# Spectral layer with routed experts: row stores of the last batches spaced out, a first table of twenty tiles, one layout of the first matrix

## The chip, the cores and the metric

One core of a Trainium2 chip runs the whole program. The metric is the device time of one execution in microseconds (us). The kernel before takes 1574.06 us, the median of three runs (1569.97 to 1574.5). Engines are named as in the profile: PE does matrix products, ACT and DVE work on whole tiles, POOL sends rows by indirect DMA, SP issues the other DMAs.

## What is computed

Two layers follow each other. The first transforms eight batches of 2496 tokens and 256 columns along the tokens, mixes the columns in the frequency domain, shrinks the result by 0.01 and transforms back. The second picks one of eight experts for each token and applies two matrices of that expert.

```python
X = np.fft.rfft(x, axis=1)
Yr = Xr @ w_r - Xi @ w_i + b_r
Yi = Xr @ w_i + Xi @ w_r + b_i
...
y = np.fft.irfft(Y, n=x.shape[1], axis=1)
...
expert_idx = np.argmax(x @ w_gate, axis=1)
h = np.maximum(xe @ w1[e], 0.0)     # 256 -> 1024
out[mask] = gate_w[mask, None] * (h @ w2[e])
```

## The kernel before

The program has two stages that overlap a little. In the **spectral stage** (`spectral`, 80 iterations, ten for each batch) a batch is transformed, mixed and transformed back. `route` then finds, for half a batch at a time, each token's expert and its place in that expert's list in DRAM (`xs_dram`). It leaves a generator of eleven **row stores** in `self.rows`: each is one indirect DMA of POOL (L646) that writes up to 117 rows of 1056 bytes to their places. `send(1)` lets one of them go, and `pace(after)` ahead of it makes POOL copy one number of the tile `after` (`mark`, L577), so that the store waits until that tile is there.

In the **expert stage** the lists are worked off in tiles of 256 rows. `step(t)` is a tile: it issues the load of tile t + 4 (`load`), then `up` multiplies by the first matrix, in four pieces of two column blocks each, and `down` multiplies by the second matrix, in two halves of 128 rows. Every product is three PE matmuls, since numbers are split in a rounded part and a rest. For each piece of `up`, ACT makes `hh` from the sum in PSUM (L923) and DVE makes the rest `hl` (L924); only then is the PSUM buffer free again. The sums have two buffers (pool `psa`) while the inverse transform still holds its share of PSUM, and four from tile `BUSY` on, when `psb` is opened. `down` ends with ACT's `part` (L958), DVE's `o` (L959) and an indirect DMA of POOL to `out` (L961), for each half.

`finish_last` is the seam. It interleaves the inverse transform of the last batch (`inv_a`, twelve steps), the routing of that batch and the tiles 0 to `BUSY - 1`. `step` is a generator that gives way after each piece of `up` and each half of `down` (in tiles 0 and 1 also in the middle of a half), and each time `breathe` does three steps of routing and sends one row store:

```python
def breathe(self, after):
    self.tick(3)
    self.nudge()
    self.pace(after)
    self.send(1)
```

Which expert and which rows a tile has is not known to the program before it runs. `table(0)` computes it for the first `EARLY` tiles, from lists of the first five batches, in which these tiles are already full. So their loads don't wait for later row stores. `table(1)` has all other tiles, and the load of tile `EARLY` (in `step(EARLY - 4)`) waits until every row store has landed. Column 1 of a table says whether a tile has another expert than the one before; then `split1` and `split2` make both matrices anew from `r1` and `r2` (eight ACT copies, L851 and L857, and eight DVE subtractions, L852 and L858), else a branch jumps over them. The first tile of a table always counts as another expert.

The first four tiles (`PLAIN`) have a **layout** of their own. Their rows are loaded by one DMA each into `xw`, and PE turns them with four transposes into PSUM (`px`, L886). From tile 4 on, four DMAs fetch pieces of 256 bytes into `xq`, a fifth fetches weight and token number into `xr`, and DVE turns 32 x 32 blocks (L890). The rows of the first matrix lie in another order for that, so the table also calls for new matrices at tile 4 (the last column of `tcol`), whatever its expert.

The order on PE, ACT, DVE and SP is the order of the code; POOL runs in program order too.

Of the kernel before, what the change touches and what calls it, by code (L numbers as in the profile page):

```python
# [10 lines left out]
F32 = mybir.dt.float32  # L11
# [17 lines left out]
XW = 264  # L29
# [2 lines left out]
OOB = 1 << 20  # L32
RARE = 3
ROUND = 1.5 * 2.0 ** 23
EARLY = 12
PLAIN = 4
BUSY = 8


def constants(nb):  # L40
    n1 = np.arange(NA)
    n2 = np.arange(NB)
    k2 = np.arange(NB)
    fa = np.zeros((117, 120))
    fe = np.zeros((78, 120))
    ga = np.zeros((120, 117))
    for j in range(3):
        for k1 in range(K1):
            ph = 2 * np.pi * ((n1 * k1) % NA) / NA
            c, r = j * 40 + 2 * k1, slice(j * 39, (j + 1) * 39)  # L50
            for q, v in enumerate((np.cos(ph), -np.sin(ph))):
                fa[j::3, (2 * k1 + q) * 3 + j] = v
                if j < 2:
                    fe[j::2, (2 * k1 + q) * 3 + j] = v
            f = (1 if k1 == 0 else 2) / S
            ga[c, r] = f * np.cos(ph)
            ga[c + 1, r] = -f * np.sin(ph)
    bm = np.zeros((128, K1, 128))
    bi = np.zeros((128, K1, 128))
    for k1 in range(K1):  # L60
        k = k1 + NA * k2
        s = np.where(k > S // 2, -1.0, 1.0)
        th = 2 * np.pi * ((n2[:, None] * k[None, :]) % S) / S
        c, z = np.cos(th), np.sin(th)
        bm[:64, k1, :64] = c
        bm[64:, k1, :64] = z
        bm[:64, k1, 64:] = -z * s
        bm[64:, k1, 64:] = c * s
        live = (((k != 0) & (k != S // 2)) * s)[:, None]
        bi[:64, k1, :64] = c.T  # L70
        bi[64:, k1, :64] = -z.T * live
        bi[:64, k1, 64:] = z.T
        bi[64:, k1, 64:] = c.T * live
    cap = TT + nb * S
    nt = (nb * S + E * (TT - 1)) // TT
    p = np.arange(117)
    g = np.arange(G)
    n2o = p[:, None] // NA + 3 * g[None, :]
    tok = NB * (p[:, None] % NA) + n2o
    ok = n2o < NB  # L80
    ids = np.where(ok[:, None, :], tok[:, None, :] + S * np.arange(nb)[None, :, None], OOB)
    score = np.broadcast_to((8.0 - np.arange(E))[None, None, :], (117, G, E)) * ok[:, :, None]
    base = np.broadcast_to((np.arange(E) * cap + TT)[None, :], (128, E))
    ltri = (p[:, None] < p[None, :]).astype(np.float64)
    tcol = np.stack([np.arange(128.0), np.arange(128.0) - 1, np.where(np.arange(128) == 0, 1.0, 0.0),
                     np.arange(128.0), np.arange(128.0) + 128,
                     np.where(np.arange(128) % PLAIN == 0, 1.0, 0.0) * (np.arange(128) <= PLAIN)], 1)
    return {
        "c_fa": fa.astype(np.float32),
        "c_fe": fe.astype(np.float32),  # L90
        "c_ga": ga.astype(np.float32),
        "c_bm": bm.astype(np.float32),
        "c_bi": bi.astype(np.float32),
        "c_ids": np.ascontiguousarray(ids.astype(np.int32)),
        "c_score": np.ascontiguousarray(score.astype(np.float32)),
        "c_base": np.ascontiguousarray(base.astype(np.float32)),
        "c_ltri": ltri.astype(np.float32),
        "c_tcol": tcol.astype(np.float32),
    }


class Kernel:
# [35 lines left out]
    def open_inverse(self, st, pst):  # L138
        nc, nb = self.nc, self.nb
        cp = self.cp  # L140
# [12 lines left out]
        nc.vector.memset(self.used, 0.0)  # L153
        self.tabs = [cp.tile([1, 4, 128], I32, name=f"tab{i}") for i in range(2)]
        self.drop = cp.tile([128, 128, 2], I32, name="drop")
        self.tcol = cp.tile([128, 6], F32, name="tcol")

        k = self.k = self.pool(st, "k", 1)
        self.wi = self.pool(st, "wi", 3)
# [385 lines left out]
            if next(self.tabling, "wait") == "wait":  # L545
                break

    def breathe(self, after):
        self.tick(3)
        self.nudge()  # L550
        self.pace(after)
        self.send(1)

    def finish_last(self):
        tiles = itertools.chain.from_iterable(self.step(t) for t in range(BUSY))
        fill = itertools.chain(self.first1(), self.first2())
        for i in range(GH + 1):
            self.inv_a(self.nb - 1, i)
            if i:
                self.pace(self.yb[0:1, (2 * i - 1) % GH, 8:9])  # L560
                self.send(1)
            else:
                for _ in self.upright(0):
                    pass
            for _ in range(2 if 0 < i < 3 else 1):
                next(fill, None)
            self.breathe(next(tiles) if i > 2 else self.h1.bitcast(F32)[0:1, 0, 0:1])
        self.jobs.append(self.table(1))
        for after in tiles:
            self.breathe(after)  # L570
        while self.jobs:
            self.tick(1)
        self.send(100)

    def pace(self, after):
        if self.rows:
# [84 lines left out]
    def table(self, last):  # L661
        nc, rt = self.nc, self.rt
# [42 lines left out]
        nc.vector.tensor_scalar_min(fin[:, 0:2], fin[:, 0:2], float(E - 1))  # L705
        nc.vector.tensor_tensor(out=fin[:, 2:3], in0=fin[:, 0:1], in1=fin[:, 1:2], op=ALU.is_gt)
        yield
        nc.vector.tensor_max(fin[:, 1:2], fin[:, 2:3], tcol[:, 2:3] if last else tcol[:, 5:6])
        nc.vector.tensor_scalar(out=te, in0=st0, scalar1=tcol[:, 0:1], scalar2=-1.0, op0=ALU.subtract, op1=ALU.mult)
        yield  # L710
        nc.vector.scalar_tensor_tensor(out=ind, in0=te, scalar=0.0, in1=ge, op0=ALU.is_ge, op1=ALU.subtract)
# [44 lines left out]
    def open_early(self):  # L756
        self.xst.close()
        k2 = self.pool(self.top, "k2", 1)
        self.r1 = [k2.tile([128, F], F32, name=f"r1{q}") for q in range(2)]
        self.r2 = [k2.tile([128, 4, D], F32, name=f"r2{q}") for q in range(2)]  # L760
        self.xws = [k2.tile([128, 2, XW], F32, name=f"xw{t}") for t in range(PLAIN)]
        self.xqs, self.xrs, self.xts, self.hs, self.new = {}, {}, {}, {}, {}
        self.weights(0, 1)
        self.weights(0, 2)
        for t in range(PLAIN):
            self.load(t)

    def open_experts(self, st):
# [13 lines left out]
    def load(self, t):  # L782
        if t >= self.nt:
            return
        nc = self.nc
        row = self.word(2, t, E * self.cap - TT)
        rows = self.xs[bass.ds(row, TT), :]
        tc = self.tc

        def fetch(dst, src):  # L790
            i = nc.sync.dma_start(dst, src)
            if PLAIN <= t < self.early:
                tc.declare_no_dep(i.ins, group="xs", reason="rows of the first batches, behind the first tile's load")
            if t < self.early:
                tc.add_to_no_dep_group("early", i.ins)

        if t < PLAIN:
            fetch(self.xws[t], rows.rearrange("(h p) c -> p h c", h=2))
            self.xrs[t] = self.xws[t]
            return  # L800
        xq = self.w2p.tile([128, 8, 2, 32], F32, tag="xq", name="xq", bufs=5)
        for q in range(4):
            fetch(xq[32 * q:32 * q + 32].rearrange("p t c i -> p t (c i)"),
                  rows[:, 8 + 64 * q:72 + 64 * q].rearrange("(t j) c -> j t c", t=8))
        xr = self.w2p.tile([128, 2, 2], F32, tag="xr", name="xr", bufs=6)
        fetch(xr, rows[:, 0:2].rearrange("(h p) c -> p h c", h=2))
        self.xqs[t], self.xrs[t] = xq, xr

    def weights(self, t, which):
# [3 lines left out]
        e = self.word(0, t, E - 1)  # L813
        ch = self.word(1, t, 1)
        for q in range(2):
            if which == 1 and t < PLAIN:
                parts = [(self.r1[q], self.w1[bass.ds(e, 1), q * 128:(q + 1) * 128, :].rearrange("o p f -> p (o f)"))]
            elif which == 1:
                parts = [(self.r1[q][p * 32:p * 32 + 32],
                          self.w1[bass.ds(e, 1), p * 64 + q * 32:p * 64 + q * 32 + 32, :].rearrange("o i f -> i (o f)"))  # L820
                         for p in range(4)]
# [54 lines left out]
    def upright(self, t):  # L876
        if t >= self.nt:
            return
        nc = self.nc
        if t < PLAIN:  # L880
            xf = self.psb.tile([128, 512], F32, tag="o", name="px") if self.psb else \
                self.psi.tile([128, 512], F32, tag="u", name="px", bufs=4)
            xf = xf.rearrange("p (c h t) -> p c h t", c=2, h=2)
            for c in range(2):
                for h in range(2):
                    nc.tensor.transpose(xf[:, c, h, :], self.xrs[t][:, h, 8 + c * 128:136 + c * 128], self.ident)  # L886
            xf = xf.rearrange("p c h t -> p c (h t)")
        else:
            xf = self.w2p.tile([128, 2, 8, 32], F32, tag="xf", name="xf")
            nc.vector.transpose(xf.rearrange("p c t j -> p t c j"), self.xqs.pop(t))  # L890
            yield
            xf = xf.rearrange("p c t j -> p c (t j)")
        xh = self.w2p.tile([128, 2, TT], F32R, tag="xh2", name="xh2", bufs=2)
        xl = self.w2p.tile([128, 2, TT], F32R, tag="xl2", name="xl2", bufs=2)
        with self.tc.high_priority():
# [6 lines left out]
    def up(self, t, work=()):  # L902
# [8 lines left out]
        for f2 in range(4):  # L911
# [12 lines left out]
                nc.vector.scalar_tensor_tensor(out=hl[:, s, :], in0=p, scalar=0.0, in1=hh[:, s, :],  # L924
                                               op0=ALU.max, op1=ALU.subtract)
            next(work, None)
            yield hh.bitcast(F32)[0:1, f2 * 2, 0:1]
        self.hs[t] = (hh, hl)

    def down(self, t):  # L930
# [12 lines left out]
        for h in range(2):  # L943
# [3 lines left out]
            for f in range(8):  # L947
# [3 lines left out]
                    nc.tensor.matmul(p[:, :D], hl[:, 7, hs], w2[:, 7, 0, :], start=False, stop=False)  # L951
                nc.tensor.matmul(p, hh[:, f, hs], w2[:, f].rearrange("p a d -> p (a d)"), start=f == 0, stop=f == 7)  # L952
                if f == 3 and t < 2:
                    yield hl.bitcast(F32)[0:1, 7, 0:1]
            if not h:
                self.split1(t + 1)
            part = self.w2p.tile([128, D], F32, tag="part", name="part", bufs=2)
# [6 lines left out]
            if t or h:  # L964
                tc.declare_no_dep(i.ins, group="out", reason="every token is in one tile only")
            tc.add_to_no_dep_group("out", i.ins)
            yield part[0:1, 0:1]

    def step(self, t):
        if t + 4 <= self.nt - RARE:  # L970
# [53 lines left out]
```

## Time and profile before

| | before |
|---|---|
| median of three runs | 1574.06 us |
| the profiled execution | 1569.84 us |
| its span, first to last instruction | 1568.1 us |
| PE busy | 1522.0 us (97%) |
| DVE, ACT, POOL busy | 911.2, 781.3, 394.3 us |
| granted clock, mean | 0.992 |

A busy share is a mean over stages. To see what a change in one stage is worth, the stage has to be cut out: here tile by tile, from the first matmul of a tile's `up` to the first of the next tile's. A row of the timeline gives an instruction's start and duration and, in brackets, how long its engine sat idle ahead of it and what ended that.

### The profile page before, as it was taken

The page shows a single profiled execution, that of the slowest core. Times are in us where ns is not written, and L with a number is a line of the kernel's source. Part 1 is how long each engine was busy: PE and PEld are TensorE (multiplying, and loading weights), DVE is VectorE, ACT ScalarE, POOL GpSimd, SP SyncE. Part 2 cuts the span into 40 slices and gives each one's busy share as a digit, 9 for nine tenths or more (in the row PEclk, how much of TensorE's full clock was granted, in tenths as well). Part 3 has the DMA queues.
Part 4 walks back from the last instruction along what each step waited for, and adds up shares of the span by engine and source line. Part 5 has one row for each costly group of instructions (what it writes and reads, how often), then busy time and mean ns, then how long its engine had stood idle before and what let it go on. Part 6 is the DMA issues. An engine that isn't in the chain of part 4 may idle for free. (4 is left out here: it accounts for less than half of the span.)

```text
span 1568.1 us, 35495 instructions
## 1 busy us (share of the span) xinstructions
PE 1522.0 (97%) x10949; PEld 1401.5 (89%) x10950; DVE 911.2 (58%) x2106; ACT 781.3 (50%) x1689; POOL 394.3 (25%) x555
## 2 busy tenths in 40 slices
PE   6999999999999999899999999999999999999997
PEld 3899999999989888789899999999999999999996
DVE  3677787777778776554655445445445445446443
ACT  2667777777777675343443334334334334334332
POOL 1002433416251534631111212111111112111111
PEclk8999999999999999999999999999999999999998
DMA  8864544636453422532433213223123213122110
GB/s 242 227 191 121 167 139 140 182 110 196 118 174 97 132 59 57 157 95 72 124 106 81 67 42 99 49 47 100 46 52 90 56 42 104 44 71 74 46 45 20
DMA packets 188386, 159.96 MB, mean 102 GB/s; under 512 B 122299, under 2 KB 158817, under 8 KB 187918
## 3 DMA queue, kind: packets, MB, share of 16 engines
q1 hardware_dynamic: 168237, 113.46, 28.3%
q0 software_dynamic: 19936, 44.04, 8.4%
q8 instruction: 89, 1.46, 0.4%
q14 instruction: 124, 1.01, 0.2%
HBM read 242.02 MB, written 66.37 MB: 197 GB/s over the span
## 5 line engine op out<-in xcount | busy, mean ns | idle before, releaser
L952 PE MATMUL po<-h,hh 128*128 128x512 f32 x1312 | 462.4, 395 | 0.4 <-ACT hh L923 0.4
L918 PE MATMUL ph<-xh,h 128*128 128x256 f32 x1312 | 372.4, 284 | 8.4 <-DVE hl L924 7.5
L918 PE MATMUL ph<-xl,h 128*128 128x256 f32 x1312 | 371.4, 283 | 0.0
L918 PE MATMUL ph<-xh,l 128*128 128x256 f32 x1312 | 371.0, 283 | 0.0
L949 PE MATMUL po<-h,hl 128*128 128x256 f32 x1148 | 324.1, 282 | 0.9 <-DVE hl L924 0.7
L924 DVE SCALAR_TENSOR_TENSOR hl<-ph,hh 128x512 fp32r<-128x512 f32 x328 | 226.2, 690 | 159.0 <-ACT hh L923 121.2
L961 POOL DMA_INDIRECT out<-o,row x140 | 139.4, 996 | 656.2 <-DVE o L959 539.8
L923 ACT ACTIVATE hh<-ph 128x512 fp32r<-128x512 f32 x328 | 193.9, 598 | 213.0 <-PE ph L918 199.1
L952 PEld LDWEIGHTS po<-h,hh 128*128 128x128 f32 x1312 | 241.4, 188 | 44.3 <-ACT hh L923 0.9
L918 PEld LDWEIGHTS ph<-xh,h 128*128 128x128 f32 x1312 | 251.5, 192 | 9.9 <-DVE hl L924 8.8
L918 PEld LDWEIGHTS ph<-xh,l 128*128 128x128 f32 x1312 | 251.4, 192 | 3.7
L959 DVE SCALAR_TENSOR_TENSOR o<-po,xr,part 128x256 f32<-128x256 f32 x156 | 75.5, 484 | 304.7 <-ACTq L871 155.4
L918 PEld LDWEIGHTS ph<-xl,h 128*128 128x128 f32 x1312 | 251.5, 192 | 0.0
L958 ACT ACTIVATE part<-po,xr 128x256 f32<-128x256 f32 x156 | 73.8, 473 | 335.9 <-PE po L952 324.1
L949 PEld LDWEIGHTS po<-h,hl 128*128 128x128 f32 x1148 | 215.3, 188 | 8.0 <-DVE hl L924 3.7
L646 POOL DMA_INDIRECT xs_dram<-yb,pos x176 | 175.6, 998 | 64.2 <-issue 51.1
L366 DVE SCALAR_TENSOR_TENSOR y<-v,r 64x256 f32<-64x256 f32 x320 | 134.2, 419 | 6.9 <-ACT r L360 0.8
L390 PE MATMUL pz<-iw,z 128*120 128x136 f32 x704 | 97.0, 280 | 1.9 <-DVE zl L396 1.2
L309 PE MATMUL pb<-bm,t 128*128 128x128 f32 x640 | 86.7, 279 | 11.9 <-DMA t<-spec_dram 9.0
L382 ACT COPY z<-pv 128x256 f32<-128x256 f32 x160 | 94.2, 711 | 3.7 <-PE pv L379 1.5
L309 PEld LDWEIGHTS pb<-bm,t 128*128 128x128 f32 x640 | 80.0, 194 | 13.1 <-issue 10.8
L379 PEld LDWEIGHTS pv<-bi,y 128*128 128x128 f32 x640 | 79.8, 192 | 12.2 <-issue 7.7
(188 smaller groups left out, 2550.9 us busy)
## 6 DMA issues: line engine op xcount, KB each, us to landing
r<-moe_w SPq DMA_DIRECT2D x174, 512.0 KB
r<-moe_w SPq DMA_DIRECT2D x640, 128.0 KB
spec_dram<-ae SPq DMA_DIRECT2D x88, 240.0 KB
t<-spec_dram SPq DMA_DIRECT2D x160, 128.0 KB
xq<-xs_dram SPq DMA_DIRECT2D x316, 64.0 KB
x<-x SPq DMA_DIRECT2D x40, 384.0 KB
x<-x SPq DMA_DIRECT2D x40, 84.0 KB
xs_dram<-yb,pos POOLq DMA_INDIRECT x176
```

The lines of the kernel that those rows point to most:

```text
L309: nc.tensor.matmul(p[:, c, :, kp, :], t[:, kp, c * 128:(c + 1) * 128], self.bm[:, 2 * s + kp, :], start=True, stop=True)
L366: nc.vector.scalar_tensor_tensor(out=y[q * 64:q * 64 + 64, kp, :], in0=u[h, q, :], scalar=LAM, in1=r[h, q, :], op0=ALU.add, op1=ALU.min)
L379: nc.tensor.matmul(p[:, c, kp, :, :], y[:, kp, c * 128:(c + 1) * 128], self.bi[:, 2 * s + kp, :], start=True, stop=True)
L382: nc.scalar.copy(self.z[:, c, 0:NB, 4 * s:4 * s + 4].rearrange("p n a -> p a n"), p[:, c].rearrange("p a r n -> p (a r) n"))
L390: nc.tensor.matmul(p[:120, c * 136:(c + 1) * 136], self.z[:, c, 3 * g:3 * g + 3, :].rearrange("p j a -> p (j a)"), self.iw[:, c, :], start ...
L646: i = nc.gpsimd.indirect_dma_start(out=self.xs[:, :], out_offset=bass.IndirectOffsetOnAxis(ap=pos[:n, g:g + 1], axis=0), in_=y[:n, g, 0:XW ...
L918: nc.tensor.matmul(p[:, i, :], a[:, c, f * 128:(f + 1) * 128], v[:, c, :], start=m == 0, stop=m == 5)
L923: nc.scalar.activation(hh[:, s, :], p, AF.Relu)
L924: nc.vector.scalar_tensor_tensor(out=hl[:, s, :], in0=p, scalar=0.0, in1=hh[:, s, :], op0=ALU.max, op1=ALU.subtract)
L949: nc.tensor.matmul(p[:, :D], hl[:, f - 1, hs], w2[:, f - 1, 0, :], start=False, stop=False)
L952: nc.tensor.matmul(p, hh[:, f, hs], w2[:, f].rearrange("p a d -> p (a d)"), start=f == 0, stop=f == 7)
L961: i = nc.gpsimd.indirect_dma_start(out=self.out[:, :], out_offset=bass.IndirectOffsetOnAxis(ap=at[h], axis=0), in_=o[:, h, :], in_offset=N ...
```

## The change

Row stores: `breathe` no longer paces and sends. In `finish_last` one store goes with each step of `inv_a`, as before, and from tile 2 on `up` sends one after its second and one after its fourth piece, in the later part of the program too, until none is left. The `send(100)` at the end of `finish_last` is gone.

First table: `EARLY` is 20 instead of 12, `BUSY` 7 instead of 8.

Layout: tiles 0 to 3 are loaded and turned as all others. `PLAIN`, the four PE transposes of a tile and the call for new matrices at tile 4 are gone; the first load of the first matrix comes in eight DMAs of 128 KB instead of two of 512 KB.

```diff
-EARLY = 12
-PLAIN = 4
-BUSY = 8
+EARLY = 20
+FIRST = 4
+BUSY = 7
...
-    def breathe(self, after):
+    def breathe(self):
         self.tick(3)
         self.nudge()
-        self.pace(after)
-        self.send(1)
...
-            self.breathe(next(tiles) if i > 2 else self.h1.bitcast(F32)[0:1, 0, 0:1])
+            if i > 2:
+                next(tiles)
+            self.breathe()
         self.jobs.append(self.table(1))
-        for after in tiles:
-            self.breathe(after)
+        for _ in tiles:
+            self.breathe()
         while self.jobs:
             self.tick(1)
-        self.send(100)
...
-        nc.vector.tensor_max(fin[:, 1:2], fin[:, 2:3], tcol[:, 2:3] if last else tcol[:, 5:6])
+        nc.vector.tensor_max(fin[:, 1:2], fin[:, 2:3], tcol[:, 2:3])
...
-        if t < PLAIN:
-            fetch(self.xws[t], rows.rearrange("(h p) c -> p h c", h=2))
-            self.xrs[t] = self.xws[t]
-            return
-        xq = self.w2p.tile([128, 8, 2, 32], F32, tag="xq", name="xq", bufs=5)
+        xq = self.xws[t] if t < FIRST else self.w2p.tile([128, 8, 2, 32], F32, tag="xq", name="xq", bufs=5)
...
-        if t < PLAIN:
...
-            for c in range(2):
-                for h in range(2):
-                    nc.tensor.transpose(xf[:, c, h, :], self.xrs[t][:, h, 8 + c * 128:136 + c * 128], self.ident)
-            xf = xf.rearrange("p c h t -> p c (h t)")
-        else:
-            xf = self.w2p.tile([128, 2, 8, 32], F32, tag="xf", name="xf")
-            nc.vector.transpose(xf.rearrange("p c t j -> p t c j"), self.xqs.pop(t))
-            yield
-            xf = xf.rearrange("p c t j -> p c (t j)")
+        xf = self.w2p.tile([128, 2, 8, 32], F32, tag="xf", name="xf")
+        nc.vector.transpose(xf.rearrange("p c t j -> p t c j"), self.xqs.pop(t))
+        yield
+        xf = xf.rearrange("p c t j -> p c (t j)")
...
             next(work, None)
-            yield hh.bitcast(F32)[0:1, f2 * 2, 0:1]
+            if t > 1 and f2 % 2:
+                self.pace(hh.bitcast(F32)[0:1, f2 * 2, 0:1])
+                self.send(1)
+            yield
```

POOL in tile 2, from its second piece of `up` to its second output, before (`mark` is the pacing copy, `xs_dram` a row store, `out` an output; the two branches belong to the skipped matrices):

```order
L577 COPY mark<-hh 1x1
L646 DMA xs_dram<-yb,pos 161792x264
L577 COPY mark<-hh 1x1
L646 DMA xs_dram<-yb,pos 161792x264
L863 UNCONDITIONAL_BRANCH
L577 COPY mark<-part 1x1
L646 DMA xs_dram<-yb,pos 161792x264
L961 DMA out<-o,xw_8082 19968x256
L577 COPY mark<-part 1x1
L646 DMA xs_dram<-yb,pos 161792x264
L961 DMA out<-o,xw_8082 19968x256
```

and with the change, all of tile 2:

```order
L575 COPY mark<-hh 1x1
L644 DMA xs_dram<-yb,pos 161792x264
L575 COPY mark<-hh 1x1
L644 DMA xs_dram<-yb,pos 161792x264
L856 UNCONDITIONAL_BRANCH
L948 DMA out<-o,xi_8086 19968x256 x2
```

A tile has two row stores instead of six; tiles 2 to 13 have them, where before tiles 1 to 4 had.

SP at the end of the spectral stage, the load of tile 0, before:

```order
L780 TENSOR_LOAD tab_76
L780 ISA x2
L791 ISA
L791 DMA xw_8080<-xs_dram 128x2x264
L780 TENSOR_LOAD tab_76
```

and with the change:

```order
L779 TENSOR_LOAD tab_76
L779 ISA x2
L790 ISA
L790 DMA xq_8080<-xs_dram 32x8x64
L790 ISA
L790 DMA xq_8080<-xs_dram 32x8x64
L790 ISA
L790 DMA xq_8080<-xs_dram 32x8x64
L790 ISA
L790 DMA xq_8080<-xs_dram 32x8x64
L790 ISA
L790 DMA xi_8084<-xs_dram 128x2x2
```

One issue became five, for each of four tiles.

DVE in tile 2, after its first piece of `up`, where the rows of tile 3 are turned, with the change (`carry` and `rb` are routing):

```order
L908 SCALAR_TENSOR_TENSOR hl<-ph,hh 128x512
L874 STREAM_TRANSPOSE xf<-xq_8082 128x8x2x32
L626 TENSOR_TENSOR carry<-carry,scan_102 117x8
L628 CAST carry_b<-carry 117x8
L630 SCALAR_TENSOR_TENSOR rb<-pr,base 117x8
L908 SCALAR_TENSOR_TENSOR hl<-ph,hh 128x512
```

The second row is new on DVE; on PE the four transposes of `xw` between two pieces of `up` are gone.

## Rows read from the trace of the kernel before

**Rows 1.** The page: span, and PE's busy time.

```profile
span 1568.1 us, 35495 instructions
PE 1522.0 (97%) x10949; PEld 1401.5 (89%) x10950; DVE 911.2 (58%) x2106; ACT 781.3 (50%) x1689; POOL 394.3 (25%) x555
```

**Rows 2.** Windows: tiles 1 to 5, 7, 11, 12, 16; last, tiles 13 to 80.

```profile
core 0: us, PE busy (x) PEld busy (x) DVE busy (x) ACT busy (x) POOL busy (x), PEclk, DMA share, GB/s
618.14:630.87 12.73, 12.54 (x91) 11.32 (x89) 8.64 (x30) 4.09 (x9) 6.46 (x11) 1.00 0.15 46
630.87:647.38 16.51, 14.04 (x88) 12.75 (x87) 7.65 (x33) 3.71 (x7) 10.78 (x17) 0.90 0.38 106
647.38:663.44 16.06, 13.16 (x91) 11.46 (x90) 9.88 (x30) 5.83 (x11) 9.60 (x14) 1.00 0.75 221
663.44:677.90 14.46, 12.25 (x83) 10.79 (x82) 10.11 (x18) 8.00 (x15) 7.41 (x12) 1.00 0.65 190
677.90:690.92 13.02, 11.61 (x82) 10.69 (x80) 7.25 (x12) 5.82 (x11) 3.17 (x3) 1.00 0.18 42
702.50:714.09 11.59, 11.59 (x81) 10.70 (x80) 4.95 (x8) 3.90 (x7) 2.94 (x3) 1.00 0.20 47
748.14:760.68 12.54, 12.08 (x82) 10.62 (x80) 9.56 (x16) 7.77 (x15) 2.10 (x3) 1.00 0.79 211
760.68:772.20 11.52, 11.52 (x82) 10.67 (x80) 7.22 (x13) 5.60 (x11) 2.89 (x3) 1.00 0.23 57
806.28:817.76 11.48, 11.48 (x81) 10.63 (x80) 7.22 (x13) 5.60 (x11) 2.50 (x3) 1.00 0.20 44
772.20:1545.27 773.07, 773.07 (x5442) 723.67 (x5441) 373.51 (x668) 291.54 (x532) 135.51 (x136) 1.00 0.26 65
```

**Rows 3.** Timeline of PE: instructions that it waited for in tiles 0 to 5.

```profile
598.18 0.38 PE L404 MATMUL py<-zh,gh 120*117 120x272 f32 x1 [1.83 <-ACT yb L405]
...
636.88 0.39 PE L918 MATMUL ph<-xh,h 128*128 128x256 f32 x1 [2.46 <-DVE hl L924]
...
655.00 0.39 PE L918 MATMUL ph<-xh,h 128*128 128x256 f32 x1 [2.02 <-DVE hl L924]
...
668.17 0.38 PE L918 MATMUL ph<-xh,h 128*128 128x256 f32 x1 [1.61 <-DVE hl L924]
...
682.34 0.38 PE L918 MATMUL ph<-xh,h 128*128 128x256 f32 x1 [1.41 <-DVE hl L924]
```

**Rows 4.** Timeline of ACT: `part` in tiles 1 and 6.

```profile
633.71 0.47 ACT L958 ACTIVATE part<-po,xw 128x256 f32<-128x256 f32 x1 [5.00 <-PE px L886]
...
702.76 0.47 ACT L958 ACTIVATE part<-po,xr 128x256 f32<-128x256 f32 x1 [2.33 <-PE po L952]
```

**Rows 5.** Timeline of POOL: row stores at the end of tile 1.

```profile
629.02 0.99 POOL L646 DMA_INDIRECT xs_dram<-yb,pos  x1 [0.17 <-issue]
...
630.38 0.99 POOL L646 DMA_INDIRECT xs_dram<-yb,pos  x1 [0.18 <-issue]
```

**Rows 6.** Timeline of PE: the transposes in tile 0, the table's matmuls in tile 3.

```profile
591.71 0.60 PE L886 MATMUL px<-ident,xw 128*128 128x128 f32 x4
592.15 0.28 PE L390 MATMUL pz<-iw,z 128*120 128x136 f32 x1
...
659.43 1.03 PE L740 MATMUL pq<-ident,fin 128*1 128x128 f32 x8
660.39 0.51 PE L952 MATMUL po<-h,hh 128*128 128x512 f32 x1
```

**Rows 7.** Groups by line: DVE's transposes (busy us, mean ns, idle before).

```profile
L890 DVE STREAM_TRANSPOSE xf<-xq 128x512 f32<-128x512 f32 x79 | 55.4, 702 | 0.0
```

**Rows 8.** Timelines of SP (loads of tiles 0 to 3; a later tile's) and POOL.

```profile
546.81 4.24 SPq L791 DMA_DIRECT2D xw<-xs_dram  x4
...
690.55 1.90 SPq L791 DMA_DIRECT2D xq<-xs_dram  x4
...
565.07 0.34 POOL L577 COPY mark<-k 1x1 f32<-1x1 f32 x1 [18.05 <-ACT k L345]
```

More of the change, by code (lines that the diff above doesn't have):

```diff
@@ L85, in constants @@
     tcol = np.stack([np.arange(128.0), np.arange(128.0) - 1, np.where(np.arange(128) == 0, 1.0, 0.0),
-                     np.arange(128.0), np.arange(128.0) + 128,
-                     np.where(np.arange(128) % PLAIN == 0, 1.0, 0.0) * (np.arange(128) <= PLAIN)], 1)
+                     np.arange(128.0), np.arange(128.0) + 128], 1)
     return {
@@ L155, in open_inverse @@
         self.drop = cp.tile([128, 128, 2], I32, name="drop")
-        self.tcol = cp.tile([128, 6], F32, name="tcol")
+        self.tcol = cp.tile([128, 5], F32, name="tcol")
         k = self.k = self.pool(st, "k", 1)
@@ L760, in open_early @@
         self.r2 = [k2.tile([128, 4, D], F32, name=f"r2{q}") for q in range(2)]
-        self.xws = [k2.tile([128, 2, XW], F32, name=f"xw{t}") for t in range(PLAIN)]
+        self.xws = [k2.tile([128, 8, 2, 32], F32, name=f"xq{t}") for t in range(FIRST)]
+        self.xis = [k2.tile([128, 2, 2], F32, name=f"xi{t}") for t in range(FIRST)]
         self.xqs, self.xrs, self.xts, self.hs, self.new = {}, {}, {}, {}, {}
@@ L764, in open_early @@
         self.weights(0, 2)
-        for t in range(PLAIN):
+        for t in range(FIRST):
             self.load(t)
@@ L791, in fetch @@
             i = nc.sync.dma_start(dst, src)
-            if PLAIN <= t < self.early:
+            if FIRST <= t < self.early:
                 tc.declare_no_dep(i.ins, group="xs", reason="rows of the first batches, behind the first tile's load")
@@ L804, in load @@
                   rows[:, 8 + 64 * q:72 + 64 * q].rearrange("(t j) c -> j t c", t=8))
-        xr = self.w2p.tile([128, 2, 2], F32, tag="xr", name="xr", bufs=6)
+        xr = self.xis[t] if t < FIRST else self.w2p.tile([128, 2, 2], F32, tag="xr", name="xr", bufs=6)
         fetch(xr, rows[:, 0:2].rearrange("(h p) c -> p h c", h=2))
@@ L815, in weights @@
         for q in range(2):
-            if which == 1 and t < PLAIN:
-                parts = [(self.r1[q], self.w1[bass.ds(e, 1), q * 128:(q + 1) * 128, :].rearrange("o p f -> p (o f)"))]
-            elif which == 1:
+            if which == 1:
                 parts = [(self.r1[q][p * 32:p * 32 + 32],
@@ L879, in upright @@
         nc = self.nc
-        if t < PLAIN:
-            xf = self.psb.tile([128, 512], F32, tag="o", name="px") if self.psb else \
-                self.psi.tile([128, 512], F32, tag="u", name="px", bufs=4)
-            xf = xf.rearrange("p (c h t) -> p c h t", c=2, h=2)
-            for c in range(2):
-                for h in range(2):
-                    nc.tensor.transpose(xf[:, c, h, :], self.xrs[t][:, h, 8 + c * 128:136 + c * 128], self.ident)
-            xf = xf.rearrange("p c h t -> p c (h t)")
-        else:
-            xf = self.w2p.tile([128, 2, 8, 32], F32, tag="xf", name="xf")
-            nc.vector.transpose(xf.rearrange("p c t j -> p t c j"), self.xqs.pop(t))
-            yield
-            xf = xf.rearrange("p c t j -> p c (t j)")
+        xf = self.w2p.tile([128, 2, 8, 32], F32, tag="xf", name="xf")
+        nc.vector.transpose(xf.rearrange("p c t j -> p t c j"), self.xqs.pop(t))
+        yield
+        xf = xf.rearrange("p c t j -> p c (t j)")
         xh = self.w2p.tile([128, 2, TT], F32R, tag="xh2", name="xh2", bufs=2)
@@ L953, in down @@
                 if f == 3 and t < 2:
-                    yield hl.bitcast(F32)[0:1, 7, 0:1]
+                    yield
             if not h:
@@ L966, in down @@
             tc.add_to_no_dep_group("out", i.ins)
-            yield part[0:1, 0:1]
+            yield
     def step(self, t):
```

## The prediction, made before the changed kernel ran

> **What bounds the kernel now.** I began with the page: PE is busy 97% of the span, DVE 58% [rows 1]. So a gain has to be PE time that is lost somewhere, or PE work that goes. Where it is lost, the windows cut at tile boundaries tell [rows 2]. Tiles 13 to 80 take 773.07 us together, 11.37 each (773.07 / 68), and PE is busy all of it: no row store, table or load costs anything there. Tile 7 takes 11.59; it still has two PSUM buffers for its first product. The tiles before differ: 12.73, 16.51, 16.06, 14.46 and 13.02 us for tiles 1 to 5. The other place is tiles 11 and 12, with 12.54 and 11.52. All this stands in the 100 us around the seam.
>
> PE's own timeline then says what it waited for [rows 3]: 1.83 us in tile 0 for ACT's copy of an inverse product, 2.46 in tile 2, 2.02 in tile 3, 1.61 in tile 4 and 1.41 in tile 5, each of the last four for the `hl` that frees a PSUM buffer. These are two kinds.
>
> In tiles 4 and 5 both matrices are made anew: ACT runs 15 and 11 instructions there where tile 7 has 7 [rows 2], and the splits stand ahead of `hh` and `hl` in the queues. Tile 4 does so only because of the layout, tile 5 because another expert begins.
>
> In tile 2 nothing of that kind happens. ACT's `part` there needs only the end of tile 1's product, which was over when tile 2 began, at 630.87; it started at 633.71, 2.84 us later. In tile 7 the same step starts 0.26 us after the boundary (702.76 against 702.50) [rows 2, 4]. So the word that PE had finished came some 2.6 us late. What was going on: POOL sent row stores back to back, 1.36 us apart [rows 5], and it ran 17 and 14 instructions in tiles 2 and 3, against 3 in tile 7 [rows 2]. After the wait the granted clock is low for a while too: its mean in tile 2 is 0.90, so a fifth of it (3.3 us) ran at the lower of its two levels (1.2 instead of 2.4 GHz) and so cost some 1.6 us; this is within the 16.51. I take the burst of row stores as the cause of these delays. It is read from what coincides, and it is the step on which most hangs.
>
> **The change, part by part**, against the profiled execution (1569.84 us, span 1568.1 [rows 1]).
>
> PE transposes. Four `px` take PE 0.44 us (591.71 to 592.15) [rows 6]; four tiles, so **1.76 us** go. One DVE transpose of 0.70 us for each tile comes instead [rows 7], the same as in every later tile. DVE, busy 58% [rows 1], hides it in tiles 7 and later; in tiles 0 to 3 DVE also routes, and uncovered the four would cost 2.8 us, more than is saved. I count nothing for it, since in tile 2 DVE is busy 7.65 of 16.51 us [rows 2].
> The Trainium skill speaks against this step: "VectorE: DVE Perf Modes", rules for kernel authors, has a 128 x 128 transpose done on TensorE where a PSUM destination will do, as it does here. By that rule there is nothing to gain and the sum below would be 1.8 us smaller. The trace disagrees for this place: PE is the engine that has no time to spare.
>
> Row stores. From six in a tile to two (tile 2), and none in tile 1; in tile 0 one for each step of the inverse transform, where before several went at once. Tile 2 has 16.51 - 11.59 - 0.44 = 4.48 us above a tile with two buffers and no transposes, tile 3 has 16.06 - 11.59 = 4.47. Of tile 3, 0.96 us are the second table's matmuls (659.43 to 660.39) [rows 6], which stay. Some of the rest is routing that DVE does anyway: tile 1, without a wait, is 12.73 - 0.44 - 11.59 = 0.70 above [rows 2]. So I take 3.78 for tile 2 and 2.81 for tile 3, and half of tile 0's 1.83, since there only the bunching goes: **7.5 us**. Ends: nothing, if it was not the burst; 4.48 + 3.51 + 1.83 = 9.8 if all goes.
> The stores that move to tiles 5 to 13 cost two POOL instructions and two pacing copies a tile, on an engine that is busy 2 to 3 of 11.5 us there [rows 2]. A pacing copy makes POOL wait for `hh` of the running tile; behind it stands that tile's own output, which comes later anyway. I count nothing.
>
> New matrices at tile 4. They go: 14.46 - 11.59 = **2.87 us**. Lower end 1.6, the wait alone [rows 3]. Tile 5 keeps its new expert, with two PSUM buffers, so its 1.41 us wait stays; if half of its trouble was the work for tile 4 just before, up to 1.43 more (13.02 - 11.59) could go.
>
> The first table. It has expert changes at tiles 0, 5, 11 and 16, as the reference's routing of the first five batches gives (5, 6, 5 and 5 full tiles for the first four experts), and the second table starts at tile 20. So instead of 4, 5, 11 and 12 it is 5, 11, 16 and 20; as many less one at the start, one more later. Tiles 11 and 12 now cost (12.54 - 11.37) + (11.52 - 11.37) = 1.32 us, being neighbours: the loads for one meet those for the other (DMA share 0.79) [rows 2]. A change alone, as at tile 16 now, costs 11.48 - 11.37 = 0.11. Three alone are 0.33, so **1.0 us** goes. The load of tile 20 waits for the last row store, sent in tile 13, and is issued in tile 16; nothing stands still for that, as the wait for tile 12 shows nothing now.
>
> `BUSY` 7: tile 7 gets four PSUM buffers, 11.59 - 11.37 = **0.2 us**.
>
> Early loads. Four issues of SP, 4.24 us from 546.81 on, become twenty. A later tile's four pieces take SP 1.90 us, so with the fifth some 2.4 us a tile, 9.6 in all: done by 557. POOL sends no row store between 547 and 565 (it waits 18.05 us), and tile 0 is in work around 598 [rows 3, 8]. The six more issues for the first matrix lie ahead of that, in SP's wait for older stores. Nothing.
>
> Sum: 1.8 + 7.5 + 2.9 + 1.0 + 0.2 = 13.4 us. From the profiled execution that is 1556.4. The median of the runs stands 4.2 us higher, at 1574.06, where it would be 1560.7. I take **1559**.
>
> **The rivals.**
> *Spacing cures nothing*: the late words come from loads of `xq` or weights in the same stretch (DMA share 0.75 in tile 3), or from routing. For it: tile 1 has stores too and no wait. Against: tile 7 has the same loads and outputs. Then only 1.8 + 2.9 + 1.0 + 0.2 = 5.9 us go: 1564 to 1568.
> *The delay comes with each meeting of a row store and a load, and is now spread*: two stores, two outputs and a load fall together in every tile from 2 to 13. With two buffers (tiles 2 to 6) a tile would pay about what tiles 2 and 3 do above tile 7, 4.7 us; with four it is hidden. Five tiles are 23.5, against the 9.0 paid now in tiles 2 and 3 and the 5.9 saved elsewhere: 8.6 slower, **1583**. It decides from the fourth such tile on (3 x 4.7 = 14.1 is still below 14.9). For it: tile 3's wait has its load in flight. Against: steady tiles have outputs and loads together and lose nothing.
> *The loads of tiles 0 to 3 come late*: 256-byte pieces instead of rows of 1056. They would have to land some 30 us after their issue to hold tile 0; from there on each us is lost in full, and 10 us of it would give 1569. The Trainium skill ("DMA: Bandwidth & Descriptors", rules for kernel authors) wants many small transfers joined to large ones, and the change does the reverse; in this trace later tiles load in this way with no PE wait.
> *It doesn't do what it says*: if the table had one expert change more in tiles 1 to 6, tile 4's 2.9 us would come back, 1562.
>
> **How the numbers follow.** Forecast 0.70; spacing cures nothing 0.15; delay spread 0.06; loads late 0.03; another expert change 0.03; something not seen, either way, 0.03. About 0.3% (4.7 us) is what a measurement of this kernel can tell from no change, so faster is below 1569.3: the forecast, most of the first rival and the last, 0.84. Same: the upper part of the first rival, late loads and part of the spread delay, 0.10. Slower 0.06. All upper ends together are 1.8 + 9.8 + 4.3 + 1.0 + 0.2 = 17.1, which gives 1552.7 from the profiled execution; the first rival ends at 1568. So 1552 to 1569, which leaves out little more than the spread delay.
>
> **What would show it.** Right: tiles 2 and 3 at 12 to 13.5 us, `part` of tile 1 starting within 0.5 us of the boundary, no PE wait over 1 us in tiles 0 to 4, granted clock 1.00 in tile 2, tile 4 below 12, tiles 11 and 12 at 11.5, tile 5 still near 13. Wrong: waits of 2 us in tiles 2 to 6 at whatever spacing (then the stores were not the cause), PE waiting for `xf` or a load at the start of tile 0, or tiles 8 to 13 above 11.6.

## The result and the profile after

The changed kernel takes 1556.68 us (median of six runs, 1554.31 to 1557.69), beside 1572.69 us for the kernel before in the same comparison (1569.97 to 1575.19). The ratio is 0.9897, with a 95% interval of 0.9885 to 0.991: about 16 us, or 1.0%, faster. The profiled execution took 1556.04 us, 13.80 less than the one shown of before.

The page of after, span and busy times (it answers to [rows 1]):

```profile
span 1554.3 us, 35598 instructions
PE 1516.7 (98%) x10934; PEld 1398.6 (90%) x10934; DVE 912.2 (59%) x2102; ACT 782.2 (50%) x1689; POOL 394.8 (25%) x554
```

The span is 13.8 us shorter. PE is busy 5.3 us less; the rest of the gain is waiting that is gone.

The windows of after, one tile each, in the order tiles 1, 2, 3, 4, 5, 7, 11, 12 (they answer to [rows 2]; columns as there):

```profile
615.47:628.24 12.77, 12.23 (x87) 10.95 (x85) 9.05 (x31) 4.09 (x9) 2.41 (x4) 1.00 0.12 33
628.24:640.04 11.80, 11.80 (x85) 10.87 (x83) 8.31 (x34) 3.86 (x7) 5.28 (x7) 1.00 0.25 61
640.04:653.22 13.18, 13.15 (x92) 11.48 (x90) 7.44 (x26) 3.95 (x7) 4.70 (x6) 1.00 0.43 112
653.22:664.95 11.73, 11.70 (x84) 10.79 (x83) 7.88 (x14) 6.04 (x11) 3.76 (x6) 1.00 0.64 188
664.95:677.97 13.02, 11.61 (x81) 10.70 (x80) 7.24 (x12) 5.81 (x11) 5.27 (x7) 1.00 0.25 61
689.61:700.97 11.36, 11.36 (x82) 10.64 (x81) 4.95 (x8) 3.94 (x7) 4.36 (x6) 1.00 0.28 70
735.02:746.54 11.52, 11.52 (x82) 10.63 (x80) 7.18 (x12) 5.60 (x11) 4.91 (x7) 1.00 0.28 72
746.54:757.89 11.35, 11.35 (x81) 10.64 (x80) 4.95 (x8) 3.95 (x7) 4.37 (x6) 1.00 0.28 70
```

Set beside [rows 2]: tile 2 went from 16.51 to 11.80 us, tile 3 from 16.06 to 13.18, tile 4 from 14.46 to 11.73, tile 11 from 12.54 to 11.52. Tiles 1 and 5 did not move. In tile 2 PE is busy for the whole window and its mean granted clock is back from 0.90 to 1.00. POOL runs seven instructions there (two pacing copies, two row stores, three outputs); in before it ran 17. Tiles 0 to 4 of before send 11, 5, 7, 6 and 4 row stores, those of after 8, 1, 2, 2 and 2.

The timeline of PE in after still shows two waits over 1 us around the seam:

```profile
587.32 0.38 PE L403 MATMUL py<-zh,gh 120*117 120x272 f32 x1 [2.16 <-ACT yb L404]
...
669.38 0.39 PE L902 MATMUL ph<-xh,h 128*128 128x256 f32 x1 [1.42 <-DVE hl L908]
```

The second is tile 5's, with its new matrices and two PSUM buffers. The first, which is 0.60 us in before, lies in the inverse transform, ahead of tile 0, which begins at 591.57 us instead of 590.28; tile 0 itself fell from 27.86 to 23.90 us.

The timeline of ACT at the same place as [rows 4], the `part` of tile 1's last half:

```profile
628.41 0.47 ACT L945 ACTIVATE part<-po,xi 128x256 f32<-128x256 f32 x1 [2.35 <-PE pr L625]
```

It starts 0.17 us after tile 2 begins (628.24); in before it was 2.84. The timeline of POOL through tile 2 (`out` is an output, `xs_dram` a row store):

```profile
628.54 1.01 POOL L948 DMA_INDIRECT out<-o,xi  x1 [9.99 <-DVE o L946]
629.85 0.99 POOL L948 DMA_INDIRECT out<-o,xi  x1 [0.30 <-DVE rb L630]
632.16 0.18 POOL L575 COPY mark<-hh 1x1 f32<-1x1 f32 x1 [1.32 <-ACT hh L907]
632.99 0.92 POOL L644 DMA_INDIRECT xs_dram<-yb,pos  x1 [0.65 <-issue]
635.36 0.18 POOL L575 COPY mark<-hh 1x1 f32<-1x1 f32 x1 [1.45 <-ACT hh L907]
636.19 1.00 POOL L644 DMA_INDIRECT xs_dram<-yb,pos  x1 [0.66 <-DMA xr<-xs_dram]
638.77 1.01 POOL L948 DMA_INDIRECT out<-o,xi  x1 [1.57 <-DVE pfb L672]
641.58 0.99 POOL L948 DMA_INDIRECT out<-o,xi  x1 [1.80 <-DVE fin L704]
```

The stores now lie 3.2 us apart, and POOL waits between them. The two outputs of tile 1 still follow each other within 1.31 us, at the start of tile 2, and nothing is late behind them in this trace.

### The profile page after: what moved, and what is told of

Read it like the earlier page. It is cut to its first block, busy times and chain, and to the rows that moved or that the text cites. A ratio compares the mean times of both kernels' runs of the same rounds, so it can differ in the third digit from the quotient of the medians.

```text
span 1554.3 us, 35598 instructions
## 1 busy us (share of the span) xinstructions
PE 1516.7 (98%) x10934; PEld 1398.6 (90%) x10934; DVE 912.2 (59%) x2102; ACT 782.2 (50%) x1689; POOL 394.8 (25%) x554
## 3 DMA queue, kind: packets, MB, share of 16 engines
q14 instruction: 124, 1.02, 0.2%
## 5 line engine op out<-in xcount | busy, mean ns | idle before, releaser
L948 POOL DMA_INDIRECT out<-o,row x124 | 123.8, 998 | 581.1 <-DVE o L946 472.7
L308 PE MATMUL pb<-bm,t 128*128 128x128 f32 x640 | 86.8, 279 | 12.3 <-DMA t<-spec_dram 9.5
L308 PEld LDWEIGHTS pb<-bm,t 128*128 128x128 f32 x640 | 80.0, 195 | 13.5 <-issue 11.2
L389 PEld LDWEIGHTS pz<-iw,z 128*120 128x120 f32 x704 | 87.7, 183 | 3.5 <-DVE zl L395 1.9
```

The source lines that it names most:

```text
L308: nc.tensor.matmul(p[:, c, :, kp, :], t[:, kp, c * 128:(c + 1) * 128], self.bm[:, 2 * s + kp, :], start=True, stop=True)
L389: nc.tensor.matmul(p[:120, c * 136:(c + 1) * 136], self.z[:, c, 3 * g:3 * g + 3, :].rearrange("p j a -> p (j a)"), self.iw[:, c, :], start ...
L948: i = nc.gpsimd.indirect_dma_start(out=self.out[:, :], out_offset=bass.IndirectOffsetOnAxis(ap=at[h], axis=0), in_=o[:, h, :], in_offset=N ...
```

## The experiments

Three theories were to be told apart. **S**: row stores sent straight behind each other make words between engines late, and spacing them is most of the gain. **L**: the layout is, since it takes away the loads and new matrices at tile 4. **T**: the longer first table is. Twelve kernels ran in three sets of four, each set on a chip of its own with its own runs of the kernel before.

### First set: the parts one by one

`e_burst` is the changed kernel with the old sending (`e_spaced` is the counterpart: the kernel before, with the new sending and the table of twenty):

```diff
-    def breathe(self):
+    def breathe(self, after):
         self.tick(3)
         self.nudge()
+        self.pace(after)
+        self.send(1)
...
+        self.send(100)
...
-            if t > 1 and f2 % 2:
-                self.pace(hh.bitcast(F32)[0:1, f2 * 2, 0:1])
-                self.send(1)
-            yield
+            yield hh.bitcast(F32)[0:1, f2 * 2, 0:1]
```

> The changed kernel with the old sending of row stores (one with each breath of the seam, all gone by tile 4); layout, table of twenty and four PSUM buffers from tile 7 stay. Theory S (row stores sent back to back delay the word between engines): tile 2 again near 16 us and tile 3 near 16, tile 0 some 2 us longer, tiles 11 and 12 at 11.5 and 11.4; 1564 to 1567 us against 1556.7 of the change. Rival L (the loads and splits for tile 4's own layout did it): tiles 2 and 3 stay at 11.8 and 13.2, 1557 us.

> The kernel before with the new sending of row stores and the table of twenty that it needs; old layout with PE transposes and new matrices at tile 4. Theory S: tile 2 at 12 to 12.5, tile 3 at 13 to 13.7, tile 4 still 14.5; 1561 to 1563 us against 1572.7 before. Rival L: tiles 2 and 3 stay above 15.5, 1570 to 1572 us.

`e_layout` is the kernel before with the layout alone (the diff of the change from `PLAIN` on, with the old `EARLY`, `BUSY` and sending), `e_table20` the kernel before with one line changed:

> The kernel before with one layout for all tiles and nothing else (table of twelve, old sending). Theory S: tile 4 at 11.8, tiles 2 and 3 still 15 to 16.5, tiles 11 and 12 together 24.1; 1567 to 1569 us. Rival L: tiles 2 and 3 at 11.8 and 13.2 too, 1560 to 1562 us.

```diff
-EARLY = 12
+EARLY = 20
```

> The kernel before with the first table of twenty tiles and nothing else. Both theories: tiles 11 and 12 at 11.5 and 11.4 instead of 12.5 and 11.5, tile 20 at 11.5, the seam as before; 1571.5 to 1572 us, about the same as before.

| | median | ratio to before, 95% | tiles 0 to 4 |
|---|---|---|---|
| before (31 runs) | 1552.18 | | |
| `e_burst` | 1550.16 | 0.9987 (0.9977 to 0.9996) | 23.90, 12.35, 11.94, 13.33, 11.73 |
| `e_spaced` | 1551.32 | 0.9997 (0.9988 to 1.0007) | 24.31, 12.75, 12.13, 13.40, 13.27 |
| `e_layout` | 1549.61 | 0.9988 (0.9978 to 0.9997) | 23.90, 12.36, 11.94, 13.32, 11.73 |
| `e_table20` | 1551.58 | 0.9997 (0.9987 to 1.0006) | 24.34, 12.76, 12.12, 13.70, 13.31 |

All four expectations missed the time, for one reason that none of them had foreseen (what they said of tile 4 in `e_layout` and of tiles 11 and 12 in `e_burst` and `e_table20` came): on this chip the kernel before takes 1552.18 us, 20 less than on the first, and even with the old sending no word is late. `e_spaced` and `e_table20` differ in the sending alone, and by 0.3 us. So the set says nothing on S. It does price the other parts without delays. From `e_table20` to `e_layout` the tiles 0 to 4 lose 0.44, 0.40, 0.18, 0.38 and 1.58 us, 2.98 together: the PE transposes for tiles 1, 2 and 3, which stand in tiles 0, 1 and 2, a wait of 0.31 us in tile 3, and tile 4's new matrices. The medians differ by only 1551.58 - 1549.61 = 1.97 us; ahead of tile 0 the new layout loses time, as shown in the section on the prediction. The table of twenty gives nothing that can be measured here.

### Second set: with and without spacing where the delays exist

The next set got a chip on which the kernel before takes 1572.20 us (19 runs), as in the first comparison. `g_before` and `g_after` are the two kernels themselves, `g_burst` is `e_burst` again, and `g_four_buffers` is the changed kernel with four PSUM buffers from tile 5 on:

```diff
-BUSY = 7
+BUSY = 5
```

> The kernel before, profiled again beside the others of this set. The first four experiments ran where the kernel before takes 1552.2 us, 20 us less than in the first comparison, and none of them showed the delays in tiles 2 and 3. Theory S with a condition (bunched row stores delay the word between engines only on some chips): if this set's time of before is near 1552, tiles 2 and 3 are at 12 to 12.2 and 13.4 to 13.7 us; if it is near 1572, they are at 16 us again. Rival (the delays come and go from one execution to the next): tiles 2 and 3 do not go with the time of before.

> The changed kernel. Where before takes 1552: only the parts that don't hang on delays are left, transposes 1.8 us, matrices of tile 4 1.5 us (13.3 against 11.7), tile 7 0.2, tiles 11 and 12 0.1 to 0.2, so 1548.0 to 1549.5 us. Where before takes 1572: 1556 to 1557 as in the first comparison.

> The changed kernel with the old sending of row stores, again. Where before takes 1552: within 1.5 us of the changed kernel. Where before takes 1572: theory S 1563 to 1567 with tiles 2 and 3 at 15 us and more; rival L (layout) as the changed kernel.

> The changed kernel with BUSY 5: four PSUM buffers from tile 5 instead of tile 7. Tile 5 loses the 1.41 us wait behind its new matrices and goes from 13.0 to 11.5, tile 6 from 11.6 to 11.4: 1.5 to 1.9 us below the changed kernel. If the routing left over at tile 4 has to be done in one piece first, tile 4 grows by up to 2 us and nothing is gained.

| | median | ratio to before, 95% | tiles 0 to 5 |
|---|---|---|---|
| `g_before` | 1571.44 | 0.9991 (0.9978 to 1.0005) | 27.59, 12.72, 18.51, 16.00, 14.36, 13.02 |
| `g_after` | 1555.55 | 0.9889 (0.9867 to 0.991) | 23.90, 12.71, 11.81, 13.17, 11.75, 13.03 |
| `g_burst` | 1574.26 | 1.0015 (1.0001 to 1.0029) | 27.56, 12.38, 19.34, 17.43, 16.04, 13.02 |
| `g_four_buffers` | 1553.25 | 0.9872 (0.985 to 0.9894) | 23.90, 12.69, 11.80, 13.17, 11.73, 11.49 |

`g_burst` and `g_after` differ in the sending alone, and by 1574.26 - 1555.55 = 18.7 us; the ranges of their runs (1572.2 to 1580.97, 1554.32 to 1556.81) lie far apart. Layout and table without spacing gain nothing at all, so L and T fall as main causes: on this chip the old sending alone takes the whole gain away. That is S as far as the sending goes. The pacing copies move with the stores, so this pair doesn't show which of the two does it. Nor was the new sending with the old layout run on such a chip; whether spacing alone brings the gain is not shown.

The same kernel is `e_burst` on the chip without delays, so the two traces can be laid on each other. Windows of tiles 2, 3 and 4 in `g_burst`:

```profile
628.44:647.78 19.34, 13.89 (x85) 12.88 (x84) 8.47 (x34) 3.85 (x7) 11.21 (x17) 0.82 0.29 80
647.78:665.21 17.43, 15.30 (x92) 12.00 (x90) 7.58 (x26) 3.84 (x7) 9.27 (x14) 0.90 0.47 133
665.21:681.25 16.04, 13.61 (x84) 11.87 (x82) 7.88 (x14) 6.02 (x11) 7.79 (x12) 0.89 0.48 133
```

The same three tiles in `e_burst`:

```profile
622.50:634.44 11.94, 11.84 (x85) 10.88 (x84) 8.30 (x34) 3.97 (x7) 10.23 (x16) 1.00 0.43 120
634.44:647.77 13.33, 13.15 (x92) 11.47 (x90) 7.52 (x26) 3.96 (x7) 10.46 (x16) 1.00 0.58 162
647.77:659.50 11.73, 11.70 (x84) 10.79 (x83) 7.87 (x14) 6.04 (x11) 8.56 (x12) 1.00 0.72 206
```

PE, ACT and DVE run the same instructions in both. The DMA engines do about the same work too: in tile 2 they are busy for 0.29 of 19.34 us and for 0.43 of 11.94, 5.6 and 5.1 us. What PE waited for, one row of its timeline in `g_burst`:

```profile
637.01 0.58 PE L903 MATMUL ph<-xh,h 128*128 128x256 f32 x1 [5.45 <-DVE hl L909]
```

It waited for `hl`, and `hl` for `hh`. ACT's timeline in `g_burst`, from the start of tile 2 at 628.44:

```profile
628.61 0.47 ACT L943 ACTIVATE part<-po,xi 128x256 f32<-128x256 f32 x1 [2.05 <-PE po L937]
635.55 1.09 ACT L908 ACTIVATE hh<-ph 128x512 fp32r<-128x512 f32 x2 [6.47 <-remote]
```

and in `e_burst`, from 622.50:

```profile
622.68 0.48 ACT L943 ACTIVATE part<-po,xi 128x256 f32<-128x256 f32 x1 [2.04 <-PE pr L626]
624.27 0.60 ACT L908 ACTIVATE hh<-ph 128x512 fp32r<-128x512 f32 x1 [1.11 <-PE ph L903]
```

The instruction of ACT ahead of `hh` waits for PE and DVE. By the semaphore records of `g_burst` it ends at 635.51, just after an update of PE's at 635.48; DVE's last was at 630.60. So it is PE's word on its first piece that came late. `hh` starts 1.77 us into the tile in `e_burst` and 7.11 us in `g_burst`: 5.3 us late, and two pieces then run together (x2). PE fills its two PSUM buffers and stands for 5.45 us; when it goes on, its matmuls take 0.58 and 0.41 us instead of 0.39 and 0.28, and the granted clock of the whole tile is 0.82. That a longer wait is followed by a stretch at the lower level (1.2 instead of 2.4 GHz) repeats what before showed in tile 2.

POOL in `g_burst` up to that point:

```profile
628.22 1.00 POOL L645 DMA_INDIRECT xs_dram<-yb,pos  x1 [0.18 <-issue]
...
629.57 0.99 POOL L645 DMA_INDIRECT xs_dram<-yb,pos  x1 [0.17 <-issue]
630.87 1.01 POOL L946 DMA_INDIRECT out<-o,xi  x1 [0.30 <-DVE lg L635]
632.18 0.99 POOL L946 DMA_INDIRECT out<-o,xi  x1 [0.30 <-issue]
```

and the same in `e_burst`:

```profile
622.30 1.00 POOL L645 DMA_INDIRECT xs_dram<-yb,pos  x1 [0.18 <-issue]
...
623.65 0.99 POOL L645 DMA_INDIRECT xs_dram<-yb,pos  x1 [0.17 <-issue]
624.95 1.01 POOL L946 DMA_INDIRECT out<-o,xi  x1 [0.30 <-ACT hh L908]
626.26 0.99 POOL L946 DMA_INDIRECT out<-o,xi  x1 [0.31 <-ACT hh L908]
```

The distances agree to 0.01 us (1.35, 1.30, 1.31). So the old sending is needed for the delay in these tiles, as `g_after` shows, but on one chip it delays and on another it does not. In `g_burst` it doesn't delay everything either: row stores go out 1.36 us apart from 624.14 on, in tile 1, and tile 1 takes 12.38 us, as in `e_burst` (12.35).

`g_four_buffers` did what it was made for. Tile 5 in its windows:

```profile
668.46:679.95 11.49, 11.49 (x81) 10.63 (x80) 7.15 (x12) 5.61 (x11) 5.84 (x7) 1.00 0.28 70
```

It fell from 13.03 to 11.49 us, since two more buffers take up the work of the new matrices; tile 6 fell by 0.3. Its median of four runs, 1553.25 us, is 2.3 below that of `g_after`; the runs overlap (1551.18 to 1557.71, and 1554.32 to 1556.81), so the gain of some 1.8 us is read from the two tiles.

### Third set: which part of the burst counts

Four more kernels were meant to say what in the burst does it. `h_spaced` is `e_spaced` again; the other three change a few lines of the changed kernel:

> The kernel before with the new sending of row stores and the first table of twenty tiles, but the old layout (four PE transposes a tile in tiles 0 to 3, new matrices at tile 4). It counts if the kernel before takes about 1572 us here; where it takes about 1552, as in the first set, no delays exist and this says nothing new (ratio 0.9997 there). If the spacing is what counts: no wait of PE over 1 us in tiles 2 and 3, tiles 2 and 3 at 12.1 and 13.4 us, tile 4 at 13.3 as in the first set, so about 3 us above the changed kernel: 1558 to 1561. If the layout is needed too (the new matrices at tile 4 and the loads of tiles 0 to 3 bring the delay): tiles 2 to 4 at 15 to 18 us, 1566 to 1572.

```diff
+            elif 0 < t < 5:
+                self.pace(hh.bitcast(F32)[0:1, f2 * 2, 0:1])
...
+            if 0 < t < 5:
+                self.pace(part[0:1, 0:1])
```

> The changed kernel, with POOL's pacing copies alone (no store behind them) added to tiles 1 to 4, six a tile, as often as the kernel before had them. It counts if the kernel before takes about 1572 us here. If the stores are what delays the words between engines: as the changed kernel, 1555 to 1557, tiles 2 and 3 at 11.8 and 13.2. If it is the copies (POOL waiting for ACT and DVE again and again, or its access to SBUF): tiles 2 and 3 at 15 us or more, 1562 to 1570.

```diff
-            if t > 1 and f2 % 2:
+            if t > 1:
```

> The changed kernel with a row store after each of the four pieces of the first product from tile 2 on, so four a tile instead of two. It counts if the kernel before takes about 1572 us here. If the delay grows with how close the stores lie: tiles 2 to 6 are longer by less than in the kernel with the old sending (19.3, 17.4, 16.0 us), say 12.5 to 15 each, 1558 to 1567. If only stores straight behind each other delay (1.36 us apart): as the changed kernel, 1555 to 1557, since four pieces lie some 1.5 to 2 us apart. If their number in a tile decides: as the old sending, 1570 or more.

```diff
-            if t > 1 and f2 % 2:
+            if t > 6:
...
+            if t > 6:
+                self.pace(part[0:1, 0:1])
+                self.send(1)
```

> The changed kernel with six row stores a tile, but from tile 7 on, where the first product has four PSUM buffers; none in tiles 2 to 6. It counts if the kernel before takes about 1572 us here. If a word that is late by 3 to 6 us holds PE only for want of a buffer: four buffers hold 5.7 us of PE work (half a tile), so tiles 7 to 10 stay below 12.5 us and the time is 1554 to 1559. If the delay holds PE whatever the buffers: tiles 7 to 10 at 15 us or more, 1567 to 1575.

| | median | ratio to before, 95% |
|---|---|---|
| before (31 runs) | 1552.82 | |
| `h_spaced` | 1551.31 | 0.9991 (0.9981 to 1.0) |
| `h_marks` | 1549.62 | 0.9982 (0.9971 to 0.9993) |
| `h_four` | 1549.88 | 0.9984 (0.9975 to 0.9994) |
| `h_late` | 1549.20 | 0.9981 (0.9971 to 0.9991) |

The third chip has no delays either, so by their own condition these runs do not tell copies from stores, nor say how close stores may lie, nor whether four buffers hide a late word. Those questions stay open. What the set shows is that the rest is free: on such a chip four row stores a tile, or six, cost PE nothing. The first two tiles that send in `h_late`, 7 (five stores) and 8 (six):

```profile
681.88:693.23 11.35, 11.35 (x81) 10.64 (x80) 4.95 (x8) 3.90 (x7) 7.01 (x11) 1.00 0.33 84
693.23:704.58 11.35, 11.35 (x81) 10.64 (x80) 4.95 (x8) 3.95 (x7) 8.33 (x14) 1.00 0.40 105
```

And it gives a measure of the change on a chip without delays. The changed kernel itself did not run there, but its three close relatives lie 2.9 to 3.6 us below before, 0.2%.

## Why the prediction was right, step by step

The time fell mainly where it was forecast, at the row stores. The sum was 13.4 us; the two profiled spans differ by 13.8. The number that the sum itself gave from the profiled execution, 1556.4, was nearer than the 1559 chosen between it and the median. That the sum came so close was in part luck: the transposes gave about nothing instead of 1.8 us, and the row stores in tiles 0, 2 and 3 gave 10.7 instead of 7.5.

- **Row stores, 7.5 us.** The step on which most hung held on the chip with delays: with the old sending the rest of the change is worth nothing there (`g_burst`), and with the new one all waits of tiles 2 and 3 are gone. Tile 2 gave 4.71 us (3.78 and a transpose of 0.44 were counted), tile 3, which has no transpose, 2.88 (2.81 counted). Tile 0's share was mis-sized: half of 1.83 us was counted, but tile 0 fell by 3.96 us, 0.44 of it a transpose. The prediction's list of waits left out a second one there, 1.18 us at 608.42. The three tiles give 4.27 + 2.88 + 3.52 = 10.7 us, above the 9.8 named as the most. The low clock in tile 2 went too.
- **Transposes, 1.76 us.** This term came to nothing. The transposes for tiles 1, 2 and 3 stand in tiles 0, 1 and 2, and from `e_table20` to `e_layout` these give 1.02 us together. The transpose for tile 0 stands ahead of it, and there the assumption that the one on DVE costs nothing failed. ACT makes `xh` from it, and ACT's copies of the inverse product (`yb`), for which PE waits, stand behind `xh`. Before:

```profile
583.99 0.58 ACT L896 CAST xh<-px 128x512 fp32r<-128x512 f32 x1
...
586.02 0.38 PE L404 MATMUL py<-zh,gh 120*117 120x272 f32 x1 [0.60 <-ACT yb L405]
```

and after, where DVE turns the rows only when its own part of the inverse transform (`zl`) is done:

```profile
584.52 0.71 DVE L874 STREAM_TRANSPOSE xf<-xq 128x512 f32<-128x512 f32 x1
...
585.27 0.62 ACT L880 CAST xh<-xf 128x512 fp32r<-128x512 f32 x1 [1.15 <-DVE xf L874]
```

PE then waits 2.16 us for `yb`. From PE's first `pz` of the last inverse transform (582.07 and 582.25) to tile 0 it takes 8.21 us before and 9.32 after, 1.11 lost. All five profiled executions with the old layout need 8.2 us for this. The nine with the new one need 9.3, or 10.5 where the granted clock fell behind the wait (in four of them; it was 0.73 from 585 to 590 us in `g_after`). Tile 1 of after gains nothing: it has a PE wait of 0.35 us that was not forecast (12.77 us, while the relatives of the third set have 12.3). The doubt taken from the Trainium skill ("VectorE: DVE Perf Modes", rules for kernel authors, which would leave such transposes on TensorE) would have made this term nothing. Nothing is what came of it in sum, but by the order of the work ahead of tile 0; in tiles 0 to 2 the DVE transposes did save PE time.

- **New matrices at tile 4, 2.87 us.** It gave 2.73. But the term mixed two things: without delays the layout is worth 1.58 us there, the lower end named (1.6). The other 1.2 are lost only on the chip with delays, and seem to go with the row stores: in `g_burst` tile 4 makes no new matrices and takes 16.04 us. Tile 5 kept its 1.42 us wait, as said.
- **First table, 1.0 us.** Tiles 11 and 12 went down by 1.02 and 0.17. This price too was seen only on chips with delays: in `e_layout`, with the old table, they take 11.50 and 11.58 us, while in `g_before` they take 11.53 and 13.61. No row store is sent in these tiles, and ACT waits for the weights there, as the prediction had it (timeline of ACT in `g_before`):

```profile
763.86 0.62 ACT L857 CAST h<-r 128x512 fp32r<-128x512 f32 x1 [1.69 <-DMA r<-moe_w]
```

So bunched row stores are not the only thing that is slower on such a chip.

- **`BUSY` 7, 0.2 us**: tile 7 gave 0.23.
- **Early loads, nothing**: no load holds PE at tile 0; DVE's transpose starts as soon as DVE is free. For `xf` PE does wait, by way of `yb`, as told above. So one sign of being wrong ("PE waiting for `xf`") came in this form.

The signs of being right came: `part` 0.17 us after the boundary, clock 1.00 in tile 2, tile 4 below 12, tiles 11 and 12 at 11.5 and 11.4; tile 2, at 11.80, fell a little below its band of 12 to 13.5. No PE wait over 1 us is left in tiles 0 to 4; that of 2.16 us stands just ahead of tile 0.

Of the rivals, *spacing cures nothing* would have left tiles 2 and 3 at 16 us. *The delay spread over tiles 2 to 6* would have put each of them 4.7 us above tile 7's 11.59; they have 11.80, 13.18, 11.73, 13.02 and 11.64. *Late loads* and *one expert change more* did not come.

What the prediction did not see is that its largest term is no property of the kernel alone. It read a cause from what coincided in one trace. The old sending is that cause on the chip of the second set; on two other chips the nearest relatives of the changed kernel (`e_burst`, `h_marks`, `h_four`, `h_late`) lie only 2.0 to 3.6 us below before.

## What to carry to other kernels

When an engine starts late although its input was long finished, look at what goes out at that moment on other queues: here four to seven paced indirect DMAs a tile, 1.3 us apart, went with words up to 5.3 us late on one chip, and two a tile did no harm. Whether the DMAs or POOL's pacing copies do it is open. Spread such sends over the steady part of the work, where they cost nothing here. An engine that has time to spare on the whole may have none at one place: the transpose given to DVE stood in PE's way ahead of tile 0. Price a cure on the machine that has the illness: the edit of the sending was worth 18.7 us in the changed kernel on one chip and 0.3 in the kernel before on another, so a comparison says little until the kernel before has run beside it.

## What was not expected of the hardware

The kernel before takes 1572.2 us on one chip and 1552.2 and 1552.8 on two others. Each of these sets had one chip at one time, so chip and time are not told apart. In the tiles laid side by side above, PE, ACT and DVE run the same instructions, POOL's rhythm is the same to 0.01 us up to the delay, and the granted clock is lower only in the tiles with the waits. What on the first chip makes words late when POOL sends in bursts is open; no run here looks inside it.

The changed kernel too is slower on such a chip. The first matmul of tile 0 in `g_after`, on the chip with delays:

```profile
592.34 0.28 PE L902 MATMUL ph<-xh,h 128*128 128x256 f32 x1
```

and in `h_four`, which has the same code up to there, on a chip without:

```profile
585.02 0.28 PE L902 MATMUL ph<-xh,h 128*128 128x256 f32 x1
```

Of the 7.3 us between them, 6.1 are lost before the last inverse transform (its first `pz` stands at 581.83 and 575.70), 1.2 after that, where `g_after` has the lower clock. The loss differs from execution to execution: `g_burst` stands 3.5 us behind `h_four` at that `pz`, `g_four_buffers` 9.0. The row stores of earlier batches go out in that stage; that they cause the loss is not shown. From tile 0 on `g_after` and `h_four` take the same, 1555.0 - 592.34 = 962.7 us and 1547.3 - 585.02 = 962.3. Whether spacing those stores too would win some of it back was not tried.
